# Larger load packets for k and q, and what their order of rows asks of the other steps

## The chip, the cores and the metric

The kernel runs on one core of one Trainium2 chip. The metric is the device time of one execution in microseconds (us); the time before is 107.34 us, the median of three runs (107.32, 107.34 and 108.46).

## The reference

Eight batches, eight heads, 576 tokens, 64 channels a head. A small set of 32 learned rows `p` per head first attends to all tokens; the tokens then attend to the 32 results. The output, with the heads side by side (512 channels), goes through a mixer over the tokens:

```
p_packed = softmax(p @ k.T / 8) @ v                # 32 x 64 per head
a_out    = softmax(q @ p_packed.T / 8) @ p_packed  # 576 x 64 per head
x        = heads of a_out side by side             # 576 x 512 per batch
wq, wk   = x @ w_q, x @ w_k                        # 576 x 64
mixed    = (wq @ wk.T / 8) @ x
out      = relu(mixed) @ w_out                     # float32
```

## The kernel before

The whole program is one list of steps, ORDER (L12 to L60). Each word is a step with its batch, a part of it, its PSUM bank, and after "@" its engine (V VectorE, A ScalarE, P GpSimd, S SyncE). Every engine works through its own steps in the order of the list, so a step that waits holds up all that stand behind it on the same engine. Up to two or three batches are in flight at once.

Loads (LD, in `load`, L157) go out on GpSimd's queue, which casts float32 to bf16 on the way: k and q of a batch as one DMA each (L182, L188; the first k as the halves h0 and g0, the first and last q as halves), v as two DMAs (L179), the learned rows p in four (LD.P0 to P3), w_k and w_q as one each (LD.W0, LD.W1, L172), and w_out as one (LD.O, L174). The first batches' p rows come in float32 over SyncE's and ScalarE's queues (LD.E). Each of k, q and v has four buffers. A partition of k or q gets two pieces of 18 rows, from heads four apart (`pairs`, L146). GpSimd also does some arithmetic between its loads: AM (attention weights times reciprocals, L408) and QD (a copy). SyncE holds back all stores until the last v is there (HOLD.v7, a small DMA that reads v's buffer), and then writes the output.

The steps of one batch b that matter here, in order:

- KT (L260): VectorE transposes k in blocks of 32x32 words, a word being two bf16 values; S1 (L268): scores of p against k on TensorE. For batches 0 and 1 (DIAG) kT is the stationary operand, for the others the moving one (L287). X1: the exponential on ScalarE; TE: a transpose back, on VectorE.
- PV (L318), RC, PP, PT: the weighted sum over v, normalised, masked and transposed.
- QV (L354): VectorE transposes q like k; S2 (L376): scores of q against the packed rows; X2: exponential; RS and RR: sums and reciprocals on VectorE; AM: the product, on VectorE or GpSimd, in parts of the tokens (part 1 is tokens 256 to 511).
- QK (L339): the packed rows times w_k and w_q (`wqk`); AT (L422, L417): transposes of AM's result on TensorE, copied out by AE; WKQ (L436): wk and wq of all tokens, where the inner function wq has aT as its moving operand (L449); GM, Y, MX, MR: the mixer's small products; RL: relu; OT (L543): the product with w_out, copied out by OE and stored by ST.
- WARM (L614): filler matmuls on TensorE, on a tile of zeros.

The order around the wait that matters most in this study reads, with other steps between: on GpSimd `LD.k3 QD.0 QD.1 LD.O LD.v3 AM.1.1 LD.k4`, and on TensorE `GM.0 WARM.3 AT.1.1 S1.2 Y.0 AT.1.0`.

Of the kernel before, what the change touches and what calls it, by code (L numbers as in the profile page):

```python
# [7 lines left out]
NL, NB, NO, NE = 4, 3, 6, 2  # L8
DIAG = (0,1)
# [1 line left out]

ORDER = """  # L12
LD.E0@S LD.E1@A SET.pz0@V SET.aT0@V SET.warm@V SET.tab@A EC@A EX@V SET.v1@V SET.idf@V PB.0.2@V LD.h0
SET.v3@P LD.g0 SET.v0@P LD.v0 LD.q0 SET.mask@P PB.0.0@P PB.0.3@V KT.0.1@V KT.0.0@V PB.0.1@V
WARM.21=1 S1.0=0,2,4 X1.0.0@A WARM.5=7 PV.0.0=0,1 PV.0.1 RC.0@V QV.0.1@V PP.0.0@V PP.0.1@V LD.r0
LD.k1 LD.W1 LD.W0 SET.aff@P SET.idb@V PT.0@V QV.0.0@V WARM.11=2 S2.0.2=0,1 S2.0.0=2,3 LD.v1 LD.P3
LD.q1 LD.P2 SET.v2@V KT.1.2@V LD.P1 LD.P0 S2.0.1=4,5 X2.0.1@A X2.0.0@A X2.0.2@A RS.0.1@V SET.aT1@V
RS.0.0@V RR.0.1@V RS.0.2@V RR.0.2@V RR.0.0@V AM.0.0@V AM.0.2@V SET.aT2@V WARM.10=6 S1.1=0,1,2
X1.1.0@A WARM.6=3 PV.1.0=0,1 PV.1.1 AT.0.0=3 AT.0.2=5 LD.k2 LD.v2 LD.q2 AM.0.1@V RC.1@V PP.1.0@V
AE.0.2@V PP.1.1@V PT.1@V AT.0.1=2 WARM.3=4 QK.1=0 QKE.1@A QK.0=1 QKE.0@A AE.0.0@V LD.k3 QD.0@P  # L20
# [43 lines left out]
def kernel(  # L64
# [41 lines left out]
    const = ctx.enter_context(tc.tile_pool(name="const", bufs=1))  # L106
# [22 lines left out]
    def copy(eng, o, i):  # L129
        if eng == "A":  # L130
            nc.scalar.activation(o, i, COPY)  # L131
        elif eng == "P":
            nc.gpsimd.tensor_copy(o, i)
        else:
            nc.vector.tensor_copy(o, i)
# [4 lines left out]
    def halves(x):  # L140
        return slice(x * 64, (x + 1) * 64)

    def quarter(x):
        return slice(x * 32, (x + 1) * 32)

    def pairs(x, b):  # L146
        return x[b].rearrange("(i c) (g r) d -> (c g) i (r d)", i=2, r=RQ)

    pT = const.tile([P, 2 * B, L, 2], bf16)
    ND = max(DIAG) + 1 if DIAG else 0  # L150
    wqk = const.tile([P, 2, 2, 2, Dl], bf16, name="wqk")
    wout = const.tile([P, NJ, D], bf16)
    v_bufs = [const.tile([P, 7, W], bf16, name=f"v_sb{n}") for n in range(NL)]
    k_in = [const.tile([P, 2, RQ * Dh], bf16, name=f"k_sb{n}") for n in range(NL)]
    q_in = [const.tile([P, 2, RQ * Dh], bf16, name=f"q_sb{n}") for n in range(NL)]

    def load(x, eng):  # L157
        a, b = x[0], x[1:]
        if a in "gh":
            i = "gh".index(a)  # L160
            nc.gpsimd.dma_start(k_in[0][:, i], pairs(k, 0)[:, i])
        elif a == "P":
            c = int(b)
            src = p.rearrange("b (i c) (y l) d -> c (b i) y (l d)", i=2, y=2)
            nc.gpsimd.dma_start(pbf[quarter(c)], src[c])
        elif a == "E":
            b = int(b)
            src = p[b].rearrange("(i c) l d -> (c l) i d", i=2)
            (nc.sync if eng == "S" else nc.scalar).dma_start(p32[:, 2 * b:2 * b + 2], src)
        elif a == "W":  # L170
            w = (moe_w_k, moe_w_q)[int(b)].rearrange("(i c j e) m -> (c j) i (e m)", i=2, c=4, e=2)
            nc.gpsimd.dma_start(wqk[:, :, int(b)].rearrange("a i e m -> a i (e m)"), w)  # L172
        elif a == "O":
            nc.gpsimd.dma_start(wout, moe_w_out.rearrange("(j a) n -> a j n", a=P))  # L174
        elif a == "v":
            b = int(b)
            for i in range(2):
                src = v[b, 4 * i:4 * i + 4].rearrange("c (g r) d -> g c (r d)", r=R)
                nc.gpsimd.dma_start(v_bufs[b % NL][halves(i), 0:7:2], src)  # L179
        elif a == "k":  # L180
            b = int(b)
            nc.gpsimd.dma_start(k_in[b % NL], pairs(k, b))  # L182
        elif a == "r" or x in ("q0", "q7"):
            b, i = int(b), int(a == "q")
            nc.gpsimd.dma_start(q_in[b % NL][:, i], pairs(q, b)[:, i])
        else:
            b = int(b)
            nc.gpsimd.dma_start(q_in[b % NL], pairs(q, b))  # L188

    idb = const.tile([P, P], bf16)  # L190
    touch = const.tile([32, 4], bf16)
# [32 lines left out]
    T = {}  # L224
    T["e2"] = [const.tile([P, 5, H * L], fp32, name=f"e2_{z}") for z in range(NE)]
    T["o"] = [const.tile([P, 4, D], fp32, name=f"o_{z}") for z in range(NO)]
    idf = T["o"][NO - 3].rearrange("a t n -> a (t n)")[:, 0:P]
    pbf = T["o"][NO - 4].rearrange("a t n -> a (t n)")[:, 0:L * Dh // 4].bitcast(bf16)
    warm = T["o"][NO - 5].rearrange("a t n -> a (t n)")[:, 0:256].bitcast(bf16)
# [13 lines left out]
    def blocks(o, i):  # L243
        nc.vector.transpose(o, i)  # L244

    def EC(eng, bk):
        copy(eng, pbe, p32.rearrange("a u d -> a (u d)"))

    def EX(eng, bk):
        blocks(pe.rearrange("a u l e -> a (u l e)").bitcast(u32), pbe.bitcast(u32))  # L250

    def PX(eng, bk):
        blocks(pT.rearrange("a u (y l) e -> a (u y l e)", y=2).bitcast(u32).rearrange("a (u l) -> a l u", l=L // 2),
# [5 lines left out]

    def KT(b, x, eng, bk):  # L260
        kT = new("kT", b, [P, 2, R, 2 * GQ, 2], bufs=NE)
        xs = slice(0, 2) if x == 2 else slice(x, x + 1)
        blocks(kT[:, xs].rearrange("a x r g e -> a (x r g e)").bitcast(u32)
               .rearrange("a (x r g t) -> a x t r g", r=R, g=GQ, t=2),
               k_in[b % NL][:, xs].rearrange("a x n -> a (x n)").bitcast(u32)
               .rearrange("a (x t m) -> a x t m", t=2, m=R * GQ))

    def S1(b, eng, bk):  # L268
        kT = T["kT", b]
        if b in DIAG:  # L270
# [12 lines left out]
        for e in range(2):  # L283
            for z in range(4):
                for c in range(4):
                    i, gh = (c + z) // 2 % 2, (c + z) % 2
                    nc.tensor.matmul(T["s1", b][c // 2][quarter(2 * i + gh), c % 2],  # L287
                                     pT[quarter(c), 2 * b + i, :, e],
                                     kT[quarter(c), i, :, gh * 32:(gh + 1) * 32, e],
                                     start=e == 0, stop=e == 1)  # L290

    def X1(b, cc, eng, bk):
# [59 lines left out]
    GR = 2 * GQ  # L352

    def QV(b, i, eng, bk):  # L354
        xs = slice(0, 2) if i == 2 else slice(i, i + 1)
        qT = new("qT", b, [P, 2, S, 2])
        blocks(qT[:, xs].rearrange("a i s e -> a (i s e)").bitcast(u32)
               .rearrange("a (i r g h) -> a i h r g", g=GQ, h=2, r=R),
               q_in[b % NL][:, xs].rearrange("a i n -> a (i n)").bitcast(u32)
               .rearrange("a (i h r n) -> a i h r n", h=2, r=R, n=GQ))  # L360

    TCH = ((0, 2), (2, 4), (4, 5), (0, 4), (0, 5))

# [72 lines left out]
    def WKQ(b, c, eng, bk=None):  # L436
        aT, pqk = aT_bufs[b % NB], T["pqk", b]
        if bk:
            T["wkq_ps", b] = ps_all[:, bk[0]:bk[1] + 1, 0:NW]
        ps = T["wkq_ps", b]  # L440

        def wk(o, t):
            for i in range(2):
                nc.tensor.matmul(o, aT[:, i, t * P:(t + 1) * P], pqk[:, i, 0:Dl],
                                 start=i == 0, stop=i == 1)

        def wq(o, c0, c1):
            for i in range(2):
                nc.tensor.matmul(o, pqk[:, i, Dl:], aT[:, i, c0:c1], start=i == 0, stop=i == 1)  # L449

        if c == 2:
            wk(ps[:, 0, 384:NW], 4)
            wq(ps[:, 1, 384:NW], 576, 640)
        else:
            for t in range(2):
                wk(ps[:, c, t * Dl:(t + 1) * Dl], 2 * c + t)
            wq(ps[:, c, 128:384], c * 256, c * 256 + 256)
# [132 lines left out]
    def STF(b, t, eng, bk):  # L590
        q = nc.scalar if eng == "A" else nc.sync
        q.dma_start(orows(b)[:, :, t * D:(t + 1) * D], T["o", b][:, t])

    steps = dict(EC=EC, EX=EX, PX=PX, PB=PB, KT=KT, S1=S1, X1=X1, TE=TE, PV=PV, RC=RC, PP=PP,
                 PT=PT, QK=QK, QKE=QKE, QD=QD, QV=QV, S2=S2, X2=X2, HA=HA, RS=RS, RR=RR, AM=AM,
                 AT=AT, AE=AE, WKQ=WKQ, WE=WE, GM=GM, GE=GE, Y=Y, YE=YE, MX=MX, MR=MR, RL=RL, RLF=RLF,
                 RLR=RLR, OT=OT, OE=OE, OEF=OEF, ST=ST, STF=STF,
# [49 lines left out]
```

## Time and profile before

| What | Value |
|---|---|
| median of the three runs | 107.34 us |
| the profiled execution's own time | 106.99 us |
| its span, first to last instruction | 105.1 us |
| DMA, GpSimd's queue | 10016 packets, 15.08 MB written |
| DMA, SyncE's queue | 3632 packets, 9.50 MB |
| read from HBM, written to HBM | 30.28 MB, 9.44 MB |
| VectorE's transposes of k and q, 1152 words a partition | 1337 to 1426 ns |
| granted TensorE clock, mean | 0.993 |

The page gives the busy time of each engine: PE is TensorE's matmuls, PEld its weight loads, DVE VectorE, ACT ScalarE, POOL GpSimd, SP SyncE. A row of a timeline holds the start and the duration in us, the engine, the line, the operation with output and input, and in brackets the idle time before it and what ended that. A row of the windows view holds the stretch, its length, the busy time and the number of instructions of PE, PEld, DVE, ACT and POOL, the granted clock, the DMA engines' share and GB/s.

### The profile page before, as it was taken

The page shows a single profiled execution, that of the slowest core. Times are in us where ns is not written, and L with a number is a line of the kernel's source. Part 1 is how long each engine was busy: PE and PEld are TensorE (multiplying, and loading weights), DVE is VectorE, ACT ScalarE, POOL GpSimd, SP SyncE. Part 2 cuts the span into 40 slices and gives each one's busy share as a digit, 9 for nine tenths or more (in the row PEclk, how much of TensorE's full clock was granted, in tenths as well). Part 3 has the DMA queues.
Part 4 walks back from the last instruction along what each step waited for, and adds up shares of the span by engine and source line. Part 5 has one row for each costly group of instructions (what it writes and reads, how often), then busy time and mean ns, then how long its engine had stood idle before and what let it go on. Part 6 is the DMA issues. An engine that isn't in the chain of part 4 may idle for free.

```text
span 105.1 us, 3592 instructions
## 1 busy us (share of the span) xinstructions
PE 93.4 (89%) x1528; PEld 52.1 (50%) x1550; DVE 78.2 (74%) x149; ACT 67.5 (64%) x107; POOL 45.7 (44%) x74
## 2 busy tenths in 40 slices
PE   3994989989979999989999999999999999999920
PEld 1334544655634554655548436655457564644410
DVE  3623197988799999698798998979997989856000
ACT  5200405405866868899999897789996874648730
POOL 6899624639562235222076289124945028000000
PEclk9999999999999999999999999999999999999997
DMA  2999999999999999999999999999989999998593
GB/s 50 132 168 194 209 209 197 211 207 210 206 213 215 203 207 214 211 206 213 210 212 209 210 208 209 214 209 207 211 237 396 391 401 405 401 399 335 227 376 121
DMA packets 13935, 24.87 MB, mean 237 GB/s; under 512 B 2144, under 2 KB 7008, under 8 KB 13920
## 3 DMA queue, kind: packets, MB, share of 16 engines
q0 software_dynamic: 10016, 15.08, 80.6%
q1 hardware_dynamic: 3632, 9.50, 23.4%
q8 instruction: 12, 0.20, 0.7%
q10 hardware_dynamic: 272, 0.07, 0.3%
q14 instruction: 3, 0.02, 0.1%
HBM read 30.28 MB, written 9.44 MB: 378 GB/s over the span
## 4 chain that ended last, share of the span: by engine, by line
PE 50%; DMA 22%; DVE 10%; POOL 5%; issue 4%; ACT 4%; ACTq 0%; DVEq 0%; POOLq 0%
PE ps L543 21%; DMA q_sb<-in_q_dram 17%; PE ps L614 6%; DMA k_sb<-in_k_dram 5%; PE ps L376 4%; PE ps L318 4%; POOL a L408 3%; PE ps L277 2%; DVE qT L244 2%; PE ps L422 2%; ACT e L381 2%; PE ps L449 2%; DVE pp L326 2%; PE ps L470 2%; PE ps L495 2%
## 5 line engine op out<-in xcount | busy, mean ns | idle before, releaser
L543 PE MATMUL ps<-wout,relu 128*128 128x512 bf16 x113 | 29.5, 380 | 0.8 <-issue 0.2
L614 PE MATMUL ps<-o 128*128 128x512 bf16 x73 | 19.8, 403 | 2.2 <-DVE o L138 1.8
L408 POOL TENSOR_TENSOR a<-e,rr 128x1024 bf16<-128x1024 f32 (+2 forms) x10 | 12.5, 1262 | 17.0 <-DVE rr L402 12.5
L131 ACT ACTIVATE o<-ps 128x1024 f32<-128x1024 f32 (+2 forms) x18 | 15.7, 882 | 3.6 <-PE ps L543 3.6
L543 PEld LDWEIGHTS <-relu 128*128 128x128 bf16 x124 | 10.9, 98 | 11.9 <-issue 1.7
L381 ACT ACTIVATE e<-ps 128x256 f32<-128x256 f32 (+2 forms) x19 | 11.1, 621 | 7.3 <-PE ps L376 7.1
L506 ACT ACTIVATE relu<-ps 128x1024 bf16<-128x1024 f32 (+1 forms) x12 | 14.3, 1233 | 0.6 <-PE ps L501 0.6
L244 DVE STREAM_TRANSPOSE kT<-k_sb 128x1152 uint32<-128x1152 uint32 (+1 forms) x9 | 11.2, 1247 | 3.4 <-DMA k_sb<-in_k_dram 3.4
L179 POOL DMA_DIRECT2D v_sb<-in_v_dram x16 | 10.1, 635 | 7.5 <-DMA q_sb<-in_q_dram 2.1
L614 PEld LDWEIGHTS <-o 128*128 128x128 bf16 x82 | 7.5, 102 | 10.5 <-issue 2.3
L397 DVE TENSOR_REDUCE rs<-e 128x16 f32<-128x512 f32 (+2 forms) x13 | 10.9, 843 | 1.5 <-ACT e L381 1.4
L244 DVE STREAM_TRANSPOSE qT<-q_sb 128x1152 uint32<-128x1152 uint32 (+1 forms) x10 | 11.1, 1114 | 0.5 <-DMA q_sb<-in_q_dram 0.4
L131 ACT ACTIVATE wkq<-ps 128x448 bf16<-128x448 f32 (+1 forms) x10 | 7.1, 732 | 2.8 <-PE ps L449 1.9
L244 DVE STREAM_TRANSPOSE e<-e1T 128x576 bf16<-128x576 bf16 x12 | 8.7, 746 | 0.2 <-ACT e1T L298 0.2
L298 ACT ACTIVATE e1T<-ps 128x576 bf16<-128x576 f32 x12 | 7.4, 650 | 1.6 <-PE ps L287 1.6
L295 ACT ACTIVATE e<-ps 128x1152 bf16<-128x1152 f32 x2 | 2.3, 1130 | 9.2 <-PE ps L277 9.2
L318 PE MATMUL ps<-v_sb,e 64*64 64x192 bf16 x288 | 7.6, 245 | 0.1
L376 PEld LDWEIGHTS <-qT 64*128 64x128 bf16 x320 | 5.4, 94 | 3.1 <-DVE qT L244 2.0
L318 PEld LDWEIGHTS <-e 64*64 64x64 bf16 x288 | 5.8, 107 | 2.2 <-ACT e L295 1.0
L376 PE MATMUL ps<-ppT,qT 64*128 64x64 bf16 x320 | 6.4, 190 | 0.5 <-DVE qT L244 0.4
L449 PE MATMUL ps<-aT,pqk 128*128 128x256 bf16 (+1 forms) x48 | 6.8, 247 | 0.0
L182 POOL DMA_DIRECT2D k_sb<-in_k_dram x7 | 5.1, 734 | 3.2 <-DMA q_sb<-in_q_dram 1.8
(76 smaller groups left out, 141.0 us busy)
## 6 DMA issues: line engine op xcount, KB each, us to landing
out_dram<-o SPq DMA_DIRECT2D x14, 512.0 KB, 5.5
v_sb<-in_v_dram POOLq DMA_DIRECT2D x16, 288.0 KB, 10.7
k_sb<-in_k_dram POOLq DMA_DIRECT2D x7, 576.0 KB, 13.0
q_sb<-in_q_dram POOLq DMA_DIRECT2D x6, 576.0 KB, 14.5
q_sb<-in_q_dram POOLq DMA_DIRECT2D x4, 288.0 KB, 9.7
out_dram<-orem SPq DMA_DIRECT2D x4, 256.0 KB, 5.4
out_dram<-o SPq DMA_DIRECT2D x3, 256.0 KB, 2.7
k_sb<-in_k_dram POOLq DMA_DIRECT2D x2, 288.0 KB, 5.0
```

What stands on the lines that cost most here:

```text
L131: nc.scalar.activation(o, i, COPY)
L179: nc.gpsimd.dma_start(v_bufs[b % NL][halves(i), 0:7:2], src)
L244: nc.vector.transpose(o, i)
L318: nc.tensor.matmul(T["pv", b][halves(cc), i], lhsT, rhs, start=n == 0, stop=n == R - 1, skip_group_check=True)
L376: nc.tensor.matmul(ps[:, y, t - t0, i], lhsT, rhs, start=e == 0, stop=e == 1)
L381: nc.scalar.activation(e2[:, t0:t1].rearrange("a t (i y n) -> a y (t i) n", i=2, y=2), T["s2", b, c].rearrange("a y t i n -> a y (t i) n") ...
L397: nc.vector.tensor_reduce(rs[:, t0 * H:t1 * H], src, axis=AX, op=ADD)
L408: e.tensor_tensor(a2[:, t0:t1].rearrange("a t i (u l) -> a (t i u) l", l=L), e2v(b, c), T["rr", b][:, t0 * H:t1 * H].to_broadcast((P, (t1 ...
L449: nc.tensor.matmul(o, pqk[:, i, Dl:], aT[:, i, c0:c1], start=i == 0, stop=i == 1)
L506: nc.scalar.activation(o, i, RELU)
L543: nc.tensor.matmul(ps, lhsT, wout[:, j, :], start=j == 0, stop=j == NJ - 1)
L614: nc.tensor.matmul(ps, warm[:, 0:P], warm, start=True, stop=True)
```

## The change

k and q come with 36 rows of one head in a partition instead of two pieces of 18 rows from two heads: a whole k or q is 128 packets instead of 256. A quarter of the partitions now holds two neighbouring heads instead of heads that are four apart, and the learned rows, v, w_k, w_q and w_out are loaded in that order of heads too. For w_k and w_q this takes eight DMAs, which go in float32 over SyncE's queue into an output tile that is still unused, behind a HOLD that waits for the first v; ScalarE casts them in a new step WC. w_out comes in four DMAs on GpSimd's queue instead of one. The first p rows come in 128 packets a batch instead of 256.

The block transposes write runs of 16 words where they wrote every second word, but every fourth word for batches 0 and 1. The tokens in kT, and those of q and all that follows from it, then stand in another order. S1 of the other batches and wq read their moving operand with a rearranged access pattern that restores the order.

```
-SET.v3@P LD.g0 SET.v0@P LD.v0 LD.q0 SET.mask@P PB.0.0@P PB.0.3@V KT.0.1@V KT.0.0@V PB.0.1@V
+SET.v3@P LD.g0 SET.v0@P LD.v0 LD.q0 HOLD.v0 LD.W@S SET.mask@P PB.0.0@P PB.0.3@V KT.0.1@V KT.0.0@V PB.0.1@V
...
-LD.k1 LD.W1 LD.W0 SET.aff@P SET.idb@V PT.0@V QV.0.0@V WARM.11=2 S2.0.2=0,1 S2.0.0=2,3 LD.v1 LD.P3
+LD.k1 SET.aff@P SET.idb@V PT.0@V QV.0.0@V WARM.11=2 S2.0.2=0,1 S2.0.0=2,3 LD.v1 LD.P3
...
-LD.q1 LD.P2 SET.v2@V KT.1.2@V LD.P1 LD.P0 S2.0.1=4,5 X2.0.1@A X2.0.0@A X2.0.2@A RS.0.1@V SET.aT1@V
+LD.q1 LD.P2 SET.v2@V KT.1.2@V LD.P1 LD.P0 S2.0.1=4,5 X2.0.1@A X2.0.0@A X2.0.2@A WC@A RS.0.1@V SET.aT1@V
...
-    def pairs(x, b):
-        return x[b].rearrange("(i c) (g r) d -> (c g) i (r d)", i=2, r=RQ)
+    def rows(t, x, b, n=slice(0, 2)):
+        n = slice(n.start * RQ * Dh, n.stop * RQ * Dh)
+        nc.gpsimd.dma_start(t[:, n], x[b].rearrange("h (g r) d -> (h g) (r d)", r=2 * RQ)[:, n])
...
         elif a == "W":
-            w = (moe_w_k, moe_w_q)[int(b)].rearrange("(i c j e) m -> (c j) i (e m)", i=2, c=4, e=2)
-            nc.gpsimd.dma_start(wqk[:, :, int(b)].rearrange("a i e m -> a i (e m)"), w)
+            for n, m in enumerate((moe_w_k, moe_w_q)):
+                w = m.rearrange("(c i j e) m -> c j i (e m)", i=2, c=4, e=2)
+                for c in range(4):
+                    nc.sync.dma_start(w32[quarter(c), :, n], w[c])
         elif a == "O":
-            nc.gpsimd.dma_start(wout, moe_w_out.rearrange("(j a) n -> a j n", a=P))
+            w = moe_w_out.rearrange("(c x i a) n -> i x a c n", i=2, c=2, x=2)
+            for i in range(2):
+                for x in range(2):
+                    nc.gpsimd.dma_start(wout[halves(x), 2 * i:2 * i + 2], w[i, x])
...
-            nc.gpsimd.dma_start(k_in[b % NL], pairs(k, b))
+            rows(k_in[b % NL], k, b)
...
+    w32 = T["o"][0][:, 0].rearrange("a (i b n) -> a i b n", i=2, b=2)
...
+    def WC(eng, bk):
+        copy(eng, wqk.rearrange("a i b e m -> a (i b e m)"), w32.rearrange("a i b n -> a (i b n)"))
...
     def KT(b, x, eng, bk):
         kT = new("kT", b, [P, 2, R, 2 * GQ, 2], bufs=NE)
-        xs = slice(0, 2) if x == 2 else slice(x, x + 1)
-        blocks(kT[:, xs].rearrange("a x r g e -> a (x r g e)").bitcast(u32)
-               .rearrange("a (x r g t) -> a x t r g", r=R, g=GQ, t=2),
-               k_in[b % NL][:, xs].rearrange("a x n -> a (x n)").bitcast(u32)
-               .rearrange("a (x t m) -> a x t m", t=2, m=R * GQ))
+        turned(kT.rearrange("a i r g e -> a (i r g e)"), k_in[b % NL], x, b in DIAG)
+
+    def turned(o, t, x, plain=False):
+        ts, ns = (slice(0, 4), slice(0, 2 * W)) if x == 2 else (slice(2 * x, 2 * x + 2), slice(x * W, x * W + W))
+        o = o.bitcast(u32).rearrange("a (i r g t) -> a t r i g" if plain else "a (i r t g) -> a t r i g", i=2, r=R, t=4)
+        blocks(o[:, ts], t.bitcast(u32)[:, ns].rearrange("a (t r n) -> a t r n", r=R, n=GQ))
...
-                                     kT[quarter(c), i, :, gh * 32:(gh + 1) * 32, e],
+                                     kT[quarter(c), i, :, :, e].rearrange("a r (t h g) -> a r h g t", t=4, h=2)[:, :, gh],
...
     def QV(b, i, eng, bk):
-        xs = slice(0, 2) if i == 2 else slice(i, i + 1)
         qT = new("qT", b, [P, 2, S, 2])
-        blocks(qT[:, xs].rearrange("a i s e -> a (i s e)").bitcast(u32)
-               .rearrange("a (i r g h) -> a i h r g", g=GQ, h=2, r=R),
-               q_in[b % NL][:, xs].rearrange("a i n -> a (i n)").bitcast(u32)
-               .rearrange("a (i h r n) -> a i h r n", h=2, r=R, n=GQ))
+        turned(qT.rearrange("a i s e -> a (i s e)"), q_in[b % NL], i)
...
-                nc.tensor.matmul(o, pqk[:, i, Dl:], aT[:, i, c0:c1], start=i == 0, stop=i == 1)
+                nc.tensor.matmul(o, pqk[:, i, Dl:],
+                                 aT[:, i, c0:c1].rearrange("a (r t g) -> a r g t", t=4, g=16), start=i == 0, stop=i == 1)
```

More of the change, by code (lines that the diff above doesn't have):

```diff
@@ L153 @@
     v_bufs = [const.tile([P, 7, W], bf16, name=f"v_sb{n}") for n in range(NL)]
-    k_in = [const.tile([P, 2, RQ * Dh], bf16, name=f"k_sb{n}") for n in range(NL)]
-    q_in = [const.tile([P, 2, RQ * Dh], bf16, name=f"q_sb{n}") for n in range(NL)]
+    k_in = [const.tile([P, 2 * RQ * Dh], bf16, name=f"k_sb{n}") for n in range(NL)]
+    q_in = [const.tile([P, 2 * RQ * Dh], bf16, name=f"q_sb{n}") for n in range(NL)]
     def load(x, eng):
@@ L160, in load @@
             i = "gh".index(a)
-            nc.gpsimd.dma_start(k_in[0][:, i], pairs(k, 0)[:, i])
+            rows(k_in[0], k, 0, slice(i, i + 1))
         elif a == "P":
             c = int(b)
-            src = p.rearrange("b (i c) (y l) d -> c (b i) y (l d)", i=2, y=2)
+            src = p.rearrange("b (c i) (y l) d -> c b (i y) (l d)", i=2, y=2)
             nc.gpsimd.dma_start(pbf[quarter(c)], src[c])
@@ L167, in load @@
             b = int(b)
-            src = p[b].rearrange("(i c) l d -> (c l) i d", i=2)
-            (nc.sync if eng == "S" else nc.scalar).dma_start(p32[:, 2 * b:2 * b + 2], src)
+            src = p[b].rearrange("h (l y) d -> (h l) (y d)", y=2)
+            (nc.sync if eng == "S" else nc.scalar).dma_start(p32[:, 2 * b:2 * b + 2].rearrange("a y d -> a (y d)"), src)
         elif a == "W":
-            w = (moe_w_k, moe_w_q)[int(b)].rearrange("(i c j e) m -> (c j) i (e m)", i=2, c=4, e=2)
-            nc.gpsimd.dma_start(wqk[:, :, int(b)].rearrange("a i e m -> a i (e m)"), w)
+            for n, m in enumerate((moe_w_k, moe_w_q)):
+                w = m.rearrange("(c i j e) m -> c j i (e m)", i=2, c=4, e=2)
+                for c in range(4):
+                    nc.sync.dma_start(w32[quarter(c), :, n], w[c])
         elif a == "O":
-            nc.gpsimd.dma_start(wout, moe_w_out.rearrange("(j a) n -> a j n", a=P))
+            w = moe_w_out.rearrange("(c x i a) n -> i x a c n", i=2, c=2, x=2)
+            for i in range(2):
+                for x in range(2):
+                    nc.gpsimd.dma_start(wout[halves(x), 2 * i:2 * i + 2], w[i, x])
         elif a == "v":
@@ L177, in load @@
             for i in range(2):
-                src = v[b, 4 * i:4 * i + 4].rearrange("c (g r) d -> g c (r d)", r=R)
+                src = v[b].rearrange("(c i) (g r) d -> i g c (r d)", i=2, r=R)[i]
                 nc.gpsimd.dma_start(v_bufs[b % NL][halves(i), 0:7:2], src)
@@ L181, in load @@
             b = int(b)
-            nc.gpsimd.dma_start(k_in[b % NL], pairs(k, b))
+            rows(k_in[b % NL], k, b)
         elif a == "r" or x in ("q0", "q7"):
             b, i = int(b), int(a == "q")
-            nc.gpsimd.dma_start(q_in[b % NL][:, i], pairs(q, b)[:, i])
+            rows(q_in[b % NL], q, b, slice(i, i + 1))
         else:
             b = int(b)
-            nc.gpsimd.dma_start(q_in[b % NL], pairs(q, b))
+            rows(q_in[b % NL], q, b)
     idb = const.tile([P, P], bf16)
@@ L247, in EC @@
         copy(eng, pbe, p32.rearrange("a u d -> a (u d)"))
+    def WC(eng, bk):
+        copy(eng, wqk.rearrange("a i b e m -> a (i b e m)"), w32.rearrange("a i b n -> a (i b n)"))
     def EX(eng, bk):
-        blocks(pe.rearrange("a u l e -> a (u l e)").bitcast(u32), pbe.bitcast(u32))
+        o = pe.rearrange("a u l e -> a (u l e)").bitcast(u32)
+        blocks(o.rearrange("a (b i g y) -> a b y i g", b=2, i=2, y=2), pbe.bitcast(u32).rearrange("a (b y n) -> a b y n", b=2, y=2))
     def PX(eng, bk):
@@ L571, in hold @@
         src = {"k": k_in, "h": k_in, "q": q_in, "r": q_in, "v": v_bufs}[x[0]][b % NL]
-        src = src[64:96, 4, 0:2] if x[0] == "v" else src[64:96, 0 if x[0] == "r" else 1, 0:2]
+        src = src[64:96, 4, 0:2] if x[0] == "v" else src[64:96, W * (x[0] not in "rh"):][:, 0:2]
         z = 2 * int(x[0] == "h")
@@ L592, in STF @@
         q.dma_start(orows(b)[:, :, t * D:(t + 1) * D], T["o", b][:, t])
-    steps = dict(EC=EC, EX=EX, PX=PX, PB=PB, KT=KT, S1=S1, X1=X1, TE=TE, PV=PV, RC=RC, PP=PP,
+    steps = dict(EC=EC, WC=WC, EX=EX, PX=PX, PB=PB, KT=KT, S1=S1, X1=X1, TE=TE, PV=PV, RC=RC, PP=PP,
                  PT=PT, QK=QK, QKE=QKE, QD=QD, QV=QV, S2=S2, X2=X2, HA=HA, RS=RS, RR=RR, AM=AM,
```

## The prediction

> **What bounds the kernel now.** I read the page's busy row and slices first, then the chain of waits, then the timelines of TensorE and of the GpSimd queue, then the DMA view issue by issue. On the page:
>
> ```profile
> PE 93.4 (89%) x1528; PEld 52.1 (50%) x1550; DVE 78.2 (74%) x149; ACT 67.5 (64%) x107; POOL 45.7 (44%) x74
> ...
> DMA  2999999999999999999999999999989999998593
> ```
>
> TensorE works 93.4 of 105.1 us in an order written out by hand, 73 of its matmuls being fillers (WARM, L614) that run whatever happens. The DMA engines are full from the third microsecond to the end of the loads. Of TensorE's 11.7 idle us, 1.8 lie before its first matmul, 1.3 before S1.0 and 4.5 behind its last; only about 4 are spread over the middle. So a faster load stream can give back little, while a new wait in TensorE's order is paid in full. The chain of waits, in order of time:
>
> ```profile
> 28.12 1.05 POOL a L408
> 29.17 0.72 POOL k_sb L182
> 29.89 0.05 issue
> 29.94 17.70 DMA q_sb<-in_q_dram
> ```
>
> The chain runs over q3's transfer to 47.64, but TensorE is late for it by only 0.18 us (idle before S2.3 at 49.09). GpSimd's own timeline shows the step that I take to decide:
>
> ```profile
> 24.55 0.52 POOL L133 COPY pqk<-pqk 128x128 bf16<-128x128 bf16 x2 [0.22 <-ACT pqk L131]
> 25.02 0.74 POOL L174 DMA_DIRECT2D wout<-in_moe_w_out_dram  x1
> 25.75 1.24 POOL L179 DMA_DIRECT2D v_sb<-in_v_dram  x2
> 28.12 1.05 POOL L408 TENSOR_TENSOR a<-e,rr 128x512 bf16<-128x512 f32 x1 [1.13 <-DVE rr L402]
> ...
> 36.91 0.71 POOL L188 DMA_DIRECT2D q_sb<-in_q_dram  x1 [1.92 <-DMA k_sb<-in_k_dram]
> ...
> 39.48 0.72 POOL L182 DMA_DIRECT2D k_sb<-in_k_dram  x1 [0.47 <-DMA wout<-in_moe_w_out_dram]
> ```
>
> The reader is to see that a load issue on this queue waits for the landing of an earlier load that has nothing to do with its buffer: q4 for k3, k5 for wout. I numbered the queue's 42 loads in order and took each landing from the DMA view (issue plus time to landing). From the 13th load on, wherever a load waits for a landing, it is the landing of the load eight places before it: q1 for q0, P1 for k1, k2 for W0, q2 for P3, k3 for q1, q4 for k3, k5 for wout, q5 for q3. So at most eight loads are open. It isn't bytes: P1 (16.88) waited with about 2 MB open, while q4 went out making 3.4 MB.
>
> TensorE around that multiply (step AM.1.1 on POOL, L408):
>
> ```profile
> 28.36 0.81 PE L614 MATMUL ps<-o 128*128 128x512 bf16 x3
> 29.23 0.40 PE L422 MATMUL ps<-idb,a 128*128 128x128 bf16 x4
> 29.75 0.48 PE L287 MATMUL ps<-kT,pT 32*32 32x288 bf16 x32
> 30.16 0.25 PE L480 MATMUL ps<-pp,g 64*64 64x128 bf16 x4
> 30.94 0.40 PE L422 MATMUL ps<-idb,a 128*128 128x128 bf16 x4 [0.54 <-DVE a L408]
> ```
>
> AM.1.1 ends at 29.17, and AT.1.1 (L422) starts at 29.23: no slack.
>
> **The change, part by part.**
>
> *LD.O in four DMAs, W off the queue.* Counted from the last p load (P0, landed 24.4), v3's second half was the eighth load behind it (k2, v2 twice, q2, k3, wout, v3 twice) and needed only P0's landing. With wout as four loads it is the eleventh and must wait for the third one behind P0: v2's second half. That landed at 20.50 + 10.6 = 31.1. From a landing to the next issue the queue's rows show 0.2 to 0.6 us; I take 0.35. Then the issue (half of 1.24, 0.63), the handover to AM.1.1 (0.05), AM.1.1 itself (1.05) and 0.06 to TensorE: 31.1 + 0.35 + 0.63 + 0.05 + 1.05 + 0.06 = 33.2, against 29.23. TensorE stands still for **4.0 us** in front of AT.1.1, with S1.2, Y.0 and everything behind it queued. What gives some back: VectorE's AM.1.0 and AM.1.2 do not need TensorE and are done by then, so the 0.54 us before AT.1.0 vanish; ScalarE, though, must do AE.1.1, YE.0, X1.2 and AE.1.2 after the stall, and by its rows (0.60 + 0.38 + 1.19 + 0.30) PV.2 comes some 3.5 us late. At S2.3 the 0.18 us wait for q3 goes. Behind that nothing on TensorE waits for a load: **3.3 us** reach the end. The load stream itself doesn't starve: at each issue several loads of 0.6 MB are still open. Behind AM.1.1, k4 goes out at about 34 instead of 29.1, but its predecessors keep the engines full until 42. POOL's issues: two fewer for W (0.74 + 0.73), three more for wout (0.5 to 0.74 each by its rows); both are inside waits that POOL has anyway.
>
> *W over SP, HOLD.v0, WC.* HOLD waits for v0's second half, which landed at 11.0. Then the touch (0.63) and eight issues at 0.44 (SP's row for the first p load): the last at 15.2, landed 2.0 us later (that load) to 4.5 (the touch at 75.8, under load), 17.2 to 19.7. SP has nothing else before 75.8. WC costs ScalarE 0.60 (its 128x512 rows) and fits the 2.08 us idle before X1.1 at 19.57, or delays X1.1 by up to 0.7. Meanwhile W takes DMA time from r0, k1 and v1 and returns what its own 1.05 us (landings 16.6 to 17.65) took; KT.1 may be 0.6 later. All this delays TensorE before 29.2, where it will stand until 33.2 anyway: nothing. Without that cover, 0.7 to 1.3.
>
> *36-row packets.* Windows cut at the landings: while k or q lands (18-row packets) the engines move 203 to 214 GB/s, mean 209; while v lands (9-row packets), 212 to 216.
>
> ```profile
> 31.20:33.90 2.70, 2.52 (x34) 1.13 (x32) 2.25 (x6) 1.84 (x6) 0.63 (x1) 1.00 1.11 212
> 33.90:36.70 2.80, 2.72 (x62) 1.67 (x64) 2.57 (x7) 2.44 (x3) 0.61 (x1) 1.00 1.19 206
> ...
> 39.30:42.20 2.90, 2.90 (x14) 1.32 (x15) 2.71 (x6) 2.56 (x4) 1.43 (x2) 1.00 1.16 215
> ```
>
> The last column (GB/s) is q2, k3, v3. Twice the packet brought no rate, so I take 0 for twice more. By landings instead (2.71 us for a k or q, 2.97 for a v) a packet costs at most 16 ns, and 8 fewer per engine save 0.13 us a tensor: 0.4 us by v2's landing, which would shorten the stall by as much. Bounds: -0.4 to +0.2.
>
> *Block transposes.* 128x576 words take 0.74 to 0.78, 128x1152 1.34 to 1.39, 128x128 in straight runs 0.31: one word per 1.0 ns, whether the written step is one word or two. So runs of 16 gain nothing. For batches 0 and 1 the step becomes four words. The nearest row is pT, step 16 words: 1.03 us for 512 words where the line through the others gives 0.70, 0.65 ns a word more. So 0 to 0.37 us for KT.0.0 (on the start's path, 8.14) and 0 to 0.75 for KT.1; before 29.2 again, so nothing. The p loads in fewer packets end before a wait for h0 (0.51): nothing.
>
> *Moving operands.* S1 and wq now read with an inner step of 64 and 32 bytes. No row shows TensorE doing that. With 4-byte steps it runs at full rate (two L449 matmuls of 256 columns in 0.22 us). Lower bound 0; upper bound pT's 0.65 ns a column: 1152 columns of wq a batch, seven batches behind the stall, 5.2 us, and 576 per S1, six times, 2.2 us. I take 0, since the nearest row by engine and operand is TensorE's own; the rest is a rival. [...]
>
> **Sum.** 106.99 (profiled execution) + 3.3 = 110.3; the median shown is 0.35 above it: **110.6 us**.
>
> **Rivals.**
> *Slow moving reads* (stall as above). [...] For: pT. Against: 4-byte steps are free.
> *The clock falls in the stall.* At the end the granted clock drops to 0.50 at about 103.6, 3.0 us after the last matmul, and the stall is 4.0. Restart: the first 6 fillers take 2.18 us, the next 9 take 2.00. A stretch of about 3.4 us at half rate costs 1.7: 112.3. [...]
> *No new wait* (the other side). If the limit is not eight loads, or v2 landed by 27, AM.1.1 keeps 28.12; the packets may then give up to 0.13 x 7 = 0.9 us at q3, of which TensorE can use 0.2 to 0.5: 106.9, from 105.8 to 108. It decides once AM.1.1 starts before about 28.5. Against it: every wait read above.
>
> **How the numbers follow.** Stall with free moving reads 0.43 (109.0 to 111.6); slow reads 0.32; clock 0.11; no new wait 0.14, half of it faster by over 1%, half within. One per cent is about what a measurement of this kernel can tell from no change. The range 108.9 to 114.7 leaves out the no-wait case and the top of the slow reads.
>
> **What would show it.** POOL's AM.1.1 at about 32 instead of 28.12, TensorE idle about 4 us before L422 near 29, put down to POOL; q3 landing within 0.9 us of 47.6; two 256-column wq matmuls in 0.22 us (free) or 0.4 (slow); S1's 32 matmuls in 0.4 or 0.65; transposes at 1.34 to 1.39. I am wrong if POOL issues v3 without waiting for v2, or if wq slows.

## The result, and the profile after

The changed kernel takes 127.62 us (median of 4 runs, 126.88 to 128.16) against 107.62 (4 runs of the kernel before, 107.32 to 108.46): a ratio of 1.184, 95% interval 1.174 to 1.194. Here and below a time is the median of all executions of a kernel, while ratios and intervals leave out those more than 1.5% above its fastest. The profiled execution took 127.32 us over a span of 125.4. The direction is as predicted; the size, 20 us instead of 3, is not, and lies outside the range.

The page of the kernel after, busy times, clock and DMA slices:

```profile
PE 110.8 (88%) x1528; PEld 54.8 (44%) x1550; DVE 80.3 (64%) x149; ACT 68.8 (55%) x108; POOL 44.0 (35%) x75
...
PEclk9999999967999999999999999999999999999999
DMA  2999999999999999999912999997989205354494
```

TensorE issues as many matmuls as before and is busy 17.4 us longer (110.8 against 93.4). The DMA engines, full without a break before, now run empty twice in the later half. So TensorE itself has become the bound. Which matmuls grew is read from the groups, kept apart by form; in each row the last figures are the busy us in all and the mean ns of one. Before:

```profile
L449 PE MATMUL ps<-aT,pqk 128*128 128x256 bf16 x32 | 6.1, 273 | 0.0
...
L287 PE MATMUL ps<-kT,pT 32*32 32x288 bf16 x192 | 2.9, 290 | 0.1
```

After:

```profile
L457 PE MATMUL ps<-aT,pqk 128*128 128x256 bf16 x32 | 16.6, 608 | 0.0
...
L299 PE MATMUL ps<-kT,pT 32*32 32x288 bf16 x192 | 7.0, 646 | 0.0
```

These are the same instructions on tiles of the same size; before, wq read neighbouring values, 2 bytes apart, and S1 every second one, 4 bytes apart. Only the pattern in which wq (L457) and S1 (L299) read their moving operand is new: an inner step of 32 and of 64 bytes. Matmuls overlap (two of wq's, 273 ns each by the row before, go by in 0.22 us together), so their price on the path is read from the chain of waits, which takes an overlap once (start, length, what). One batch's wq and the last S1, after:

```profile
90.88 1.10 PE ps L299 x30
...
94.62 0.22 PE ps L457 x2
94.84 0.12 PE ps L452 x4
94.96 0.88 PE ps L457 x2
```

Before:

```profile
75.51 0.41 PE ps L287 x20
...
77.62 0.22 PE ps L449 x2
77.90 0.06 PE ps L449 x2
78.07 0.22 PE ps L449 x2
```

A pair of 256 columns takes 0.88 instead of 0.22 us, a pair of 64 columns 0.22 instead of 0.06: 2 x 0.66 + 0.16 = 1.48 us a batch. S1 takes 1.10 instead of 0.41, 0.69 more. Over eight and six batches that is 11.8 + 4.1 = 15.9 us.

The rest is lost early. The chain of the kernel after, in order of time, starts with the small weights:

```profile
4.55 6.78 DMA v_sb<-in_v_dram
11.35 5.81 DMA touch<-v_sb
17.17 6.03 DMA o<-in_moe_w_q_dram
23.35 0.63 ACT wqk L131
23.98 1.03 ACT e L307
25.05 0.94 PE ps L330 x36
```

The timeline of SyncE's queue says why the chain goes through the touch, HOLD's small DMA:

```profile
11.35 0.63 SPq L583 DMA_DIRECT2D touch<-v_sb  x1
12.02 1.98 SPq L175 DMA_DIRECT2D o<-in_moe_w_k_dram  x4
14.04 3.44 SPq L175 DMA_DIRECT2D o<-in_moe_w_q_dram  x4
```

The last of the eight issues starts only as the touch lands, at 17.17, and lands at 23.2. WC stands in front of X1.1 on ScalarE and X1.1 in front of PV.1 on TensorE, so PV.1 comes at 25.05 instead of 20.87. TensorE idles 2.23 us for it, and about a microsecond later its granted clock drops. The windows view of the kernel after (the clock is the third column from the end):

```profile
25.00:26.00 1.00, 0.95 (x38) 0.80 (x39) 0.00 (x0) 0.00 (x0) 0.39 (x1) 1.00 1.01 204
26.00:27.00 1.00, 0.78 (x11) 0.72 (x13) 0.83 (x4) 0.00 (x0) 0.00 (x0) 0.64 1.07 194
27.00:28.00 1.00, 1.00 (x4) 0.17 (x3) 0.97 (x4) 0.00 (x0) 0.00 (x0) 0.50 1.14 196
```

At half clock QK.1 takes 1.06 us instead of 0.63 and six fillers 1.81 instead of 1.47; the first wk, batch 0's, comes at 31.94 instead of 26.55, 5.4 us late. Adding up to AT.1.1: S1.0 is 0.8 late (10.02 against 9.22), S1.1 1.9 (20.16, 18.28), PV.1 4.2, wk 5.4, AT.1.1 6.6 (35.82, 29.23; batch 0's slow wq is the last 1.2). The first two of these are no measure of the change: in the profiled kernels of this study that keep the old transposes, S1.1 begins anywhere from 18.28 to 20.12 (20.44 in s1, where the clock falls ahead of it), and the kernel before is the earliest of them. Behind AT.1.1 seven wq and six S1 remain: 7 x 1.48 + 6 x 0.69 = 14.5 us, where the span grew by 20.3 - 6.6 = 13.7. The sum closes within 0.8.

And the stall in front of AT.1.1, the heart of the prediction, is not there. GpSimd's timeline after:

```profile
29.53 0.53 POOL L133 COPY pqk<-pqk 128x128 bf16<-128x128 bf16 x2 [4.14 <-ACT pqk L131]
30.00 2.38 POOL L180 DMA_DIRECT2D wout<-in_moe_w_out_dram  x4
32.33 1.27 POOL L185 DMA_DIRECT2D v_sb<-in_v_dram  x2
33.57 1.12 POOL L416 TENSOR_TENSOR a<-e,rr 128x512 bf16<-128x512 f32 x1
```

GpSimd stood at QD.0 until 29.53, because the packed rows need the late weights. By the time it came to v3, v2's second half was about to land (issued 21.77, 9.6 us under way: 31.4, where 31.1 was predicted), and v3 went out without a wait that shows. AM.1.1 is over at 34.69, before TensorE asks for it at 35.82.

### The profile page after: what moved, and what is told of

It is laid out like the page before. It is cut to its first block, busy times and chain, and to the rows that moved or that the text cites. A ratio compares the mean times of both kernels' runs of the same rounds, so it can differ in the third digit from the quotient of the medians.

```text
span 125.4 us, 3611 instructions
## 1 busy us (share of the span) xinstructions
PE 110.8 (88%) x1528; PEld 54.8 (44%) x1550; DVE 80.3 (64%) x149; ACT 68.8 (55%) x108; POOL 44.0 (35%) x75
## 4 chain that ended last, share of the span: by engine, by line
PE 67%; DMA 15%; ACT 4%; POOL 4%; DVE 3%; issue 3%; ACTq 0%; DVEq 0%; POOLq 0%
PE ps L552 21%; PE ps L457 13%; DMA v_sb<-in_v_dram 5%; PE ps L299 5%; PE ps L623 5%; DMA o<-in_moe_w_q_dram 5%; DMA touch<-v_sb 5%; PE ps L330 4%; PE ps L430 3%; PE ps L384 3%; PE ps L504 3%; PE ps L452 3%; PE ps L479 2%; PE ps L351 2%; POOL a L416 2%
## 5 line engine op out<-in xcount | busy, mean ns | idle before, releaser
L623 PE MATMUL ps<-o 128*128 128x512 bf16 x73 | 21.2, 425 | 2.4 <-DVE o L138 1.8
L457 PE MATMUL ps<-aT,pqk 128*128 128x256 bf16 (+1 forms) x48 | 18.6, 498 | 0.0
L389 ACT ACTIVATE e<-ps 128x256 f32<-128x256 f32 (+2 forms) x19 | 11.1, 620 | 7.2 <-PE ps L384 6.9
L251 DVE STREAM_TRANSPOSE kT<-k_sb 128x1152 uint32<-128x1152 uint32 (+1 forms) x9 | 12.8, 1420 | 3.3 <-DMA k_sb<-in_k_dram 3.3
L131 ACT ACTIVATE wkq<-ps 128x448 bf16<-128x448 f32 (+1 forms) x10 | 7.3, 731 | 13.6 <-PE ps L457 11.8
L623 PEld LDWEIGHTS <-o 128*128 128x128 bf16 x82 | 8.0, 107 | 12.0 <-issue 4.5
L251 DVE STREAM_TRANSPOSE qT<-q_sb 128x1152 uint32<-128x1152 uint32 (+1 forms) x10 | 11.1, 1106 | 0.0
L133 POOL COPY pqk<-pqk 128x128 bf16<-128x128 bf16 x8 | 2.3, 297 | 18.9 <-ACT pqk L131 18.9
L452 PEld LDWEIGHTS <-aT 128*128 128x128 bf16 x80 | 5.5, 103 | 7.8 <-issue 5.5
L452 PE MATMUL ps<-pqk,aT 128*128 128x64 bf16 x80 | 6.5, 195 | 0.7 <-DVE aT L135 0.5
```

Of the source, the lines that this page charges most:

```text
L389: nc.scalar.activation(e2[:, t0:t1].rearrange("a t (i y n) -> a y (t i) n", i=2, y=2), T["s2", b, c].rearrange("a y t i n -> a y (t i) n") ...
L457: nc.tensor.matmul(o, pqk[:, i, Dl:], aT[:, i, c0:c1].rearrange("a (r t g) -> a r g t", t=4, g=16), start=i == 0, stop=i == 1)
L623: nc.tensor.matmul(ps, warm[:, 0:P], warm, start=True, stop=True)
```

## The experiments

Two theories stood after the trace. By A the moving reads cost at the end all that their rows say. By B a good part of that is covered by other lateness, and less comes back when they are undone. The first four kernels undo the change one part at a time, each on top of the last; where a read is straight, the order of the tokens is not restored.

### The wq reads straight (e1_wq_straight)

```
-  aT[:, i, c0:c1].rearrange("a (r t g) -> a r g t", t=4, g=16), start=i == 0, stop=i == 1)
+  aT[:, i, c0:c1], start=i == 0, stop=i == 1)
```

> The kernel after, with wq reading its moving operand straight again (the order of the tokens in wq is then not restored, so that part of the output is another). Theory A, slow moving reads: in the trace after, a pair of 256-column wq matmuls took 0.88 us against 0.22, a pair of 64 columns 0.22 against 0.06, so 1.48 us a batch; all eight batches give it back: 127.6 - 11.8 = 115.8 us, and a pair takes 0.22 us again. Rival B, the slow reads lie largely beside other engines' work: at most half comes back, 121 to 122 us.

Measured: 116.48 us (115.14 to 117.30), 1.073 of before (1.062 to 1.084). 11.1 us below the change, or 12.0 over the executions that the ratio uses (116.05 and 115.14), where eight batches of 1.48 give 11.8: theory A's number, and about five below B's.

### The S1 reads straight too (e2_both_straight)

```
-  kT[quarter(c), i, :, :, e].rearrange("a r (t h g) -> a r h g t", t=4, h=2)[:, :, gh],
+  kT[quarter(c), i, :, gh * 32:(gh + 1) * 32, e],
```

> As the run before, and S1 of batches 2 to 7 also reads straight (order not restored there either). Theory A: S1 goes from 1.10 to 0.41 us, six times 0.69 = 4.1 us: 111.7 us. What is left over the kernel before, about 4 us, is then the late small weights (X1.1 at 23.9 instead of 19.6) and the slower transposes of batches 0 and 1. Rival B: 118 or more.

Measured: 112.21 us, 1.038 (1.028 to 1.047): another 4.3 us, by the rows 4.1. What is left, 4.8 us over before, holds no slow read. The small weights are as late as in the change: WC runs at 23.41, PV.1 at 25.12 after 2.67 us of idle time, and the granted clock goes to 0.50 again from 27 to 30.

### No HOLD in front of the small weights (e4_straight_no_hold)

```
-SET.v3@P LD.g0 SET.v0@P LD.v0 LD.q0 HOLD.v0 LD.W@S SET.mask@P ...
+SET.v3@P LD.g0 SET.v0@P LD.v0 LD.q0 LD.W@S SET.mask@P ...
```

(on top of the last kernel)

> Straight reads in wq and S1 as before, and the small weights go out on SyncE's queue at once, without waiting for v0 (no HOLD). Theory C, the predicted wait on eight open loads: with the weights early, GpSimd gets to v3 before v2's second half has landed (31.4 in the trace after), AM.1.1 starts at about 32.4 and AT.1.1 at 33.5, so that only part of the 4 us comes back: 110.5 to 111.5 us, with a GpSimd wait for v2's landing in the trace. Rival D, no such wait: AT.1.1 at 30 to 30.5, 107.5 to 108.5 us.

Measured: 109.13 us, 1.012 (1.004 to 1.019): between the two theories. The predicted wait now shows. GpSimd, then TensorE, in this kernel:

```profile
29.46 0.62 POOL L185 DMA_DIRECT2D v_sb<-in_v_dram  x1 [0.56 <-DMA v_sb<-in_v_dram]
30.87 0.61 POOL L185 DMA_DIRECT2D v_sb<-in_v_dram  x1 [0.79 <-DVE kT L251]
31.49 1.06 POOL L416 TENSOR_TENSOR a<-e,rr 128x512 bf16<-128x512 f32 x1
```

```profile
32.61 0.40 PE L430 MATMUL ps<-idb,a 128*128 128x128 bf16 x4 [2.06 <-POOL a L416]
```

The second row names a transpose, which is no input of a load; v2's second half, issued at 20.80 and 9.8 us under way, landed then. TensorE comes 1.4 us late to that place, so the stall is 2.06 us and not the 3.4 that lie between 32.61 and 29.23. The slower transposes of the first batches may be part of the 1.4, but o1 below has the old ones and comes 1.2 late.

### w_out as one load again (e5_one_wout)

```
-  for i in range(2):
-      for x in range(2):
-          nc.gpsimd.dma_start(wout[halves(x), 2 * i:2 * i + 2], w[i, x])
+  nc.gpsimd.dma_start(wout, moe_w_out.rearrange("(j a) n -> a j n", a=P))
```

(on top of the last kernel; w_out's rows then stand in the old order of heads)

> As the run before, with w_out as one load again instead of four (its rows then stand in the old order of heads, so the output is another). Theory C: v3 waits for P0 only, AM.1.1 starts by 29, and the run gains 2 to 3.5 us on the one with four loads: 107.5 to 108.5 us. Rival D: no difference between the two (within 0.5 us).

Measured: 107.55 us, 0.997 (0.990 to 1.005): the time of before. AM.1.1 starts at 29.52 and AT.1.1 at 30.62. That is theory C's time; the gain of 1.6 us on the kernel with four loads is below its 2 to 3.5, since the stall removed was 2.06. Of the 1.4 us by which TensorE is still late at AT.1.1, 0.81 come back in three waits that shrink against before: 0.54 to 0.23 in front of AT.1.0, 0.47 to 0.15 in front of a wk near 46, and 0.18 to none in front of S2.3. S2.3 starts at 49.81 instead of 49.09, and the profiled execution is as much longer (107.71, 106.99). The medians show none of it. So packets, transposes, learned rows and small weights without the HOLD together cost between -1.1 and +0.5 us (the interval). Which of them costs a little and which gives it back isn't shown, because the start of the kernel moves by more than that from one execution to the next.

### Only w_out in four loads, on the kernel before (o1_four_wout)

```
-  nc.gpsimd.dma_start(wout, moe_w_out.rearrange("(j a) n -> a j n", a=P))
+  w = moe_w_out.rearrange("(i c x a) n -> i x a c n", i=2, c=2, x=2)
+  for i in range(2):
+      for x in range(2):
+          nc.gpsimd.dma_start(wout[halves(x), 2 * i:2 * i + 2], w[i, x])
```

> The kernel before with one part of the change alone: w_out in four loads instead of one. Theory C, at most eight open loads (the prediction's step at its full size): v3's second half waits for v2's second half (31.1), AM.1.1 starts at about 32.1 instead of 28.1, TensorE stands 4 us in front of AT.1.1, and 3.3 us reach the end: 110 to 111 us. Rival D, part of it is given back, since later steps wait for the load stream anyway (q3's landing at 47.6): 108 to 109.5 us.

Measured: 111.46 us, 1.034 (1.027 to 1.042). GpSimd and TensorE of this kernel:

```profile
29.59 0.62 POOL L182 DMA_DIRECT2D v_sb<-in_v_dram  x1 [0.23 <-DMA v_sb<-in_v_dram]
31.02 0.61 POOL L182 DMA_DIRECT2D v_sb<-in_v_dram  x1 [0.81 <-DVE rr L405]
31.65 1.06 POOL L411 TENSOR_TENSOR a<-e,rr 128x512 bf16<-128x512 f32 x1
```

```profile
29.58 0.81 PE L617 MATMUL ps<-o 128*128 128x512 bf16 x3
32.76 0.40 PE L425 MATMUL ps<-idb,a 128*128 128x128 bf16 x4 [2.37 <-POOL a L411]
```

AT.1.1 is at 32.76, 0.4 us from the 33.2 of the prediction, with three more DMAs and no other change, so rival D falls; the time is a little above theory C's 110 to 111. The releaser that the second row names, RR on VectorE, is no input of a load; v2's second half landed then (issued at 21.23, 9.5 us under way), the load eight places ahead. The stall is 2.37 us and not 4.0: TensorE is through with its fillers only at 30.39 instead of 29.17, and it was late by as much at S1.1 (19.52 against 18.28), before any load of w_out went out. After the stall comes the second part, in the windows view:

```profile
34.00:35.00 1.00, 1.00 (x11) 0.40 (x8) 0.42 (x1) 1.00 (x3) 0.53 (x1) 0.54 1.15 209
35.00:36.00 1.00, 1.00 (x12) 0.45 (x8) 0.74 (x2) 0.43 (x2) 0.00 (x0) 0.50 1.19 200
```

The granted clock is 0.54, 0.50, 0.50 and 0.76 from 34 to 38: 1.70 us of full clock are missing. The lateness at AT.1.1 (3.5) and the fall make 5.2; the medians show 3.6, so about 1.6 come back later. The 0.54 in front of AT.1.0 is part of it; the rest was not traced. So the 3.6 us are near the 3.3 that the prediction gave this step, but by another sum: a shorter stall and a fall of the clock that its 3.3 left out.

### What the moving read costs by its step (five kernels)

Each is the kernel before with only wq's read changed, so that it reads the same 256 columns in another order; the order of the tokens in wq is then not the right one, and nothing else is touched. The last two keep two or four neighbouring bf16 values together.

```
-  aT[:, i, c0:c1]
+  aT[:, i, c0:c1].rearrange("a (r t g) -> a r g t", t=4, g=16)       s1: step 32 bytes
+  ... "a (r t g) -> a r g t", t=4, g=8                               s2: step 16 bytes
+  ... "a (r t g) -> a r g t", t=4, g=4                               s3: step 8 bytes
+  ... "a (t g y) -> a g t y", g=8, y=2                               s4: pairs, 32 bytes apart
+  ... "a (t g y) -> a g t y", g=4, y=4                               s5: runs of four, 32 bytes apart
```

Step 32 bytes:

> The kernel before with one part of the change alone: wq reads aT with an inner step of 32 bytes (columns of wq in another order, so the output is another). Theory A: a 256-column wq matmul goes from 0.11 to 0.44 us, 1.48 us a batch, eight batches: 107.4 + 11.8 = 119.2 us, less what the load stream hides in the first 48 us (WKQ.0 to WKQ.2): 116 to 119. Rival B, the reads are slow only together with the rest of the change: 107.4 to 109.

Step 16 bytes:

> [...] Rival M, the slowness grows with the step: 0.22 to 0.33 us a matmul.

Step 8 bytes:

> [...]

Pairs:

> [...] Rival M (it is the jump of 32 bytes that costs, once a pair): 0.28 us, half way between 0.11 and 0.44.

Runs of four:

> The kernel before, wq reading four neighbouring elements (8 bytes) in a row, the groups 32 bytes apart. So far: pairs 32 bytes apart 0.23 us a matmul, a step of 8 bytes 0.135, a step of 16 or 32 bytes 0.44. [...]

| Kernel | us | ratio to before (95%) | pair of 256 columns, us | ns a column |
|---|---|---|---|---|
| before, step 2 bytes | | 1 | 0.22 | 0.43 |
| s1, step 32 bytes | 119.23 | 1.094 (1.083 to 1.105) | 0.88 | 1.72 |
| s2, step 16 bytes | 119.08 | 1.103 (1.095 to 1.111) | 0.88 | 1.72 |
| s3, step 8 bytes | 108.30 | 1.003 (0.999 to 1.007) | 0.27 | 0.53 |
| s4, pairs | 111.13 | 1.029 (1.021 to 1.038) | 0.46 | 0.90 |
| s5, runs of four | 107.94 | 1.004 (0.999 to 1.008) | 0.24 | 0.47 |

The last column is the pair divided by 512. The pair is the first line of each fence below, from the chains of s2, s3, s4 and s5; the second is a pair of 64 columns.

```profile
92.19 0.88 PE ps L449 x2
...
93.13 0.22 PE ps L449 x2
```

```profile
92.36 0.27 PE ps L449 x2
...
92.70 0.07 PE ps L449 x2
```

```profile
93.81 0.46 PE ps L449 x2
...
94.34 0.12 PE ps L449 x2
```

```profile
91.11 0.24 PE ps L449 x2
...
91.42 0.06 PE ps L449 x2
```

s1 alone gives 10 us by its ratio and 11 by the medians, of the 20, on a kernel with none of the other parts; rival B falls. s2 equals s1, 0.44 us a matmul, so the price does not grow from a step of 16 to one of 32 bytes, and s2's rival M with 0.22 to 0.33 falls. s3 is nearly free, 0.135 us a matmul against 0.11, and takes 1.003 of the time of before: the price begins between the steps of 8 and 16 bytes. s4 jumps by 32 bytes as s1 does, but once for two values, and takes 0.23 us a matmul, half the rate of before; that is below the 0.28 of its rival M, by which the jump costs the same whatever follows it. s5 jumps as far once for four values and takes 0.12 us a matmul, nearly the rate of before.

The five runs give the price of five patterns, and the price falls with the number of neighbouring values in a row: 1.72, 0.90 and 0.47 ns a column for one, two and four at the same jump of 32 bytes. What in TensorE's read makes it so is not shown.

### Only the packets (p1_packets)

```
-        return x[b].rearrange("(i c) (g r) d -> (c g) i (r d)", i=2, r=RQ)
+        return x[b].rearrange("h (g y r) d -> (h g) y (r d)", y=2, r=RQ)
+
+    def whole(t, x, b):
+        src = x[b].rearrange("h (g r) d -> (h g) (r d)", r=2 * RQ)
+        nc.gpsimd.dma_start(t.rearrange("a i n -> a (i n)"), src)
...
-            nc.gpsimd.dma_start(k_in[b % NL], pairs(k, b))
+            whole(k_in[b % NL], k, b)
...
-            nc.gpsimd.dma_start(q_in[b % NL], pairs(q, b))
+            whole(q_in[b % NL], q, b)
```

Whole k and q on the kernel before, in 128 packets (the halves at the start and the end stay in pieces of 18 rows); the rows stand in other places than the steps take them for.

> The kernel before with whole k and q in 128 packets of 36 rows instead of 256 of 18 (the rows then stand in other places, so the output is another), and nothing else. Theory P, the packet size gives nothing at this size: loads land as before, k7 to q7 within 0.5 us, 107.3 us within 0.4. Rival Q, a packet costs 16 ns: the 14 loads that change land 1.8 us earlier in all, and the time falls by 0.2 to 0.8 us.

Measured: 107.30 us, 0.995 (0.991 to 0.999), 12 runs against 22 of the kernel before with a median of 107.82: a gain of 0.5 us, 0.1 to 0.9 by the interval. GpSimd's queue on its page:

```profile
q0 software_dynamic: 8352, 15.08, 78.1%
```

Before it was 10016 packets and 80.6% of the engines' span. Early landings come sooner: k2 at 27.7 against 28.3, k3 at 36.1 against 36.6. Late ones don't: k7 at 72.7 against 72.9, and SyncE's hold behind the last v goes out at 76.25 against 75.81. The gain speaks for rival Q and the late landings for P, so the two aren't separated.

### The small weights in seven loads (w1_seven)

On top of e2, to ask whether their lateness is the limit of eight open loads, now on SyncE's queue (touch and eight make nine):

```
-                for c in range(4):
+                for c in range(4 - 2 * n):
                     nc.sync.dma_start(w32[quarter(c), :, n], w[c])
+            nc.sync.dma_start(w32[64:128, :, 1], ...)
```

Half of w_q then comes from other rows.

> Straight reads in wq and S1, with HOLD, as the second run, but the small weights in seven DMAs instead of eight (the last two pieces of one weight as one, with other rows, so the output is another). Theory H, at most eight DMAs open on SyncE's queue too: in the second run the eighth waited for HOLD's small DMA to land at 17.2 and came in at 23.2; the seventh goes out at about 15.5 and lands at about 21.7, X1.1 starts near 22.3 instead of 23.9, 1.5 us come back, or 3 if the clock doesn't fall: 109 to 110.7 us against 112.2. Rival I, it is only the load on the DMA engines: X1.1 at 23.5 or later and no change.

Measured: 113.34 us, 1.041 (1.030 to 1.053), no better than e2's 112.21. SyncE's last issue and WC:

```profile
15.33 0.74 SPq L176 DMA_DIRECT2D o<-in_moe_w_q_dram  x1
```

```profile
24.16 0.63 ACT L131 ACTIVATE wqk<-o 128x512 bf16<-128x512 f32 x1 [5.51 <-DMA o<-in_moe_w_q_dram]
```

The last load goes out 1.8 us earlier than in the change and waits for no landing, but takes 8.8 us instead of 6.0. So the wait of the eighth is real, as theory H says, but without it nothing comes back, and H falls as the cause. What fits is rival I: beside GpSimd's full load queue, a small DMA on SyncE's queue takes 6 to 9 us. (The last one here is two pieces in one, 64 KB instead of 32, which may be part of its 8.8.) Why the engines serve it so late stays open.

## Why the prediction was wrong, step by step

Both of the prediction's own signs of being wrong came: GpSimd issued v3 without waiting for v2, and wq slowed. Taken apart in order, the 20.1 us from e5 to the change are: wq's reads 11.1, S1's reads 4.3, the small weights behind HOLD 3.1, w_out in four 1.6 (12.0, 3.8, 3.0 and 1.5 over the executions that the ratios use). The last two depend on that order: the four loads cost 3.6 us alone and less where something else is late already. The 3.1 also holds falls of the clock: e2's four executions took 110.97 us at a mean granted clock of 1.000 and up to 114.14 at 0.963.

- **"Moving operands": failed, and it is 15 of the 20 us.** "I take 0, since the nearest row by engine and operand is TensorE's own." It gave L449, wq's row, as one with 4-byte steps, which is a misreading: that row reads neighbouring values, 2 bytes apart, and TensorE's row with 4-byte steps is S1's, L287. S1 was run with no shorter step, so that 4-byte steps are free there is not shown. The change reads at steps of 32 and 64 bytes, and s3 and s2 show that the price begins between 8 and 16 (0.53 and 1.72 ns a column). The row is nearest by engine and far by pattern. The upper bound was too low as well: 0.65 ns a column more, from a VectorE row, where the runs show 1.72 - 0.43 = 1.29. The rival "Slow moving reads" had the cause, with a chance of 0.32. But its signs of 0.4 us for a pair and 0.65 for S1, and the range's top of 114.7, take a rate of these reads that no run shows: the runs show 0.88 and 1.10, for wq a quarter of the rate of before. With 1.48 us a batch for wq and 0.69 for S1 its sum is 7 x 1.48 + 6 x 0.69 = 14.5, and 13.7 of it reached the end.
- **"W over SP, HOLD.v0, WC": failed.** Landing 17.2 to 19.7 was predicted, 23.2 measured. Two us of that are the last issue, at 17.17 instead of 15.2: it waited for the touch to land, which fits the limit of eight that the prediction had read off GpSimd's queue and did not apply here. The rest is the time to landing: the predicted 2.0 us came from a p load with the engines still nearly idle and the 4.5 from the touch at 75.8; the touch took 5.8 and the weights 6.0. The text said "without that cover, 0.7 to 1.3"; here the cost (TensorE 4.2 us late at PV.1, 5.4 at wk) was larger than the cover, and the cover, the stall at 29.2, did not come.
- **"LD.O in four DMAs": right in mechanism, but not present in the changed kernel.** o1 shows it: AT.1.1 at 32.76 (33.2 predicted). That o1's 3.6 us also lie near the predicted 3.3 is in part luck: the stall was 2.4 us instead of 4.0, and a fall of the clock added 1.7. In the change, GpSimd reached v3 only when the limit no longer bound. Two delays on one path do not add; the larger one hides the other. What the step missed is that the small weights feed QD.0, which stands in front of LD.O on the same queue.
- **"The clock falls in the stall", a rival at 0.11: the price was right (1.7 us), the condition too strict.** The prediction put the fall at 3 to 4 us of idle time; it came after 2.23 in the change, 2.37 in o1, 2.67 in e2 and 2.06 in e4's profiled execution. Counted from the start of the idle stretch it came 3.5 to 4.2 us later, when work had begun again. How long a fall lasts stood in no row of the trace before; in the change the clock is at 0.50 from 26.3 to 29.7, which are the 3.4 us that the rival's 1.7 took.
- **"36-row packets": about right.** 0 taken, -0.4 to +0.2 allowed, -0.5 (-0.9 to -0.1) measured by itself.
- **"Block transposes": runs of 16 right, every fourth word slightly over the bound.** VectorE after and before, for batch 1:

```profile
17.86 2.25 DVE L251 STREAM_TRANSPOSE kT<-k_sb 128x1152 uint32<-128x1152 uint32 x1 [1.19 <-DMA k_sb<-in_k_dram]
```

```profile
16.62 1.38 DVE L244 STREAM_TRANSPOSE kT<-k_sb 128x1152 uint32<-128x1152 uint32 x1 [0.76 <-DMA k_sb<-in_k_dram]
```

The transpose takes 0.87 us more where 0.75 was the top. "Before 29.2 again, so nothing" leaned on the same missing cover; e5, with these transposes and none of the other costs, is 0.7 us late at S2.3 in its profiled execution, which the start alone can make, and not in the medians.
- **The limit of eight open loads: borne out** as a forecast by o1 and e4, where v3's two halves go out as v2's land.

Still open: why small DMAs on SyncE's queue take 6 to 9 us beside the load queue, what besides the length of an idle stretch decides whether the clock falls, and why a moving read costs from 0.43 to 1.72 ns a column by its pattern. A version of the change that restores the order with reads in runs of four values (s5's pattern, 0.24 us a pair against 0.22) or at another place was not tried. Of all that was run, only p1 has an interval below the kernel before, by 0.5 us, without the restored order.

## What to carry to other kernels

Price a rearranged operand by a row with its own pattern: over single bf16 values 16 or 32 bytes apart TensorE's moving read took 1.72 ns a column here, four times the 0.43 over neighbouring values, over pairs 32 bytes apart 0.90, over runs of four 0.47, and no row with a smaller step tells that. Where a cost is taken as hidden, price what happens if it is larger than its cover, and follow what is queued behind it: the small weights' 3 us went through ScalarE, TensorE and GpSimd, and undid the stall that was to hide them. On GpSimd's queue, where at most eight loads were open, w_out in four loads of the same bytes cost 3.6 us alone (o1) and 1.6 behind other lateness (e4 against e5); the price fell on v3, a later load, so count the loads behind the one that is split.

## What the runs showed of the hardware

- A moving bf16 operand of TensorE: 0.43 ns a column over neighbouring values (before), 0.53 at a step of 8 bytes (s3), 1.72 at 16 and 32 (s2, s1), 0.90 in pairs (s4) and 0.47 in runs of four (s5) that lie 32 bytes apart. VectorE's block transpose writes a word in about 1.2 ns in runs of 16 or every second word (1.32 to 1.43 us for 1152) and in 1.95 at every fourth (2.25 us).
- The granted clock went to 0.50 for about 3.4 us, 1.7 us of full clock each time, in seven profiled executions (the change, e1, e2, e4, o1, s1, w1), after idle stretches of 2.06 to 3.63 us. The fall came 3.0 to 4.2 us after the stretch began; in five of the seven work had begun again 1 to 2 us before. Stretches of 2.25 us (e1) and 2.13 us (w1), both in front of S1.0, passed without a fall, where one of 2.08 us at the same place in s1 brought it; so the length alone does not decide.
- It comes in some executions of a kernel and not in others: in e4 the profiled execution, with the fall, took 111.14 us at a mean granted clock of 0.984, and the other three 108.70 to 109.39 us at 0.994 to 0.998.
- HOLD's small DMA on SyncE's queue landed 5.8 us after its issue with GpSimd's load queue full, and the small weights' 6 to 9 us after theirs.
